# Attention with head mixing and a gated MLP: the second mixing and the product with v issued in turns of four matmuls

## The chip, the cores and the metric

One core of a Trainium2 chip. The metric is the device time of one execution in microseconds (us); a kernel's time is the median of its runs.

## The reference

Attention over 4 batches, 12 heads, 448 positions and 64 columns, with the heads mixed before and after the softmax; then RMS norm and a gated MLP.

```python
scores = scale * np.matmul(q, k.transpose(0, 1, 3, 2))
scores = np.einsum('bhij,hg->bgij', scores, w_pre)
scores = scores - np.max(scores, axis=-1, keepdims=True)
attn = np.exp(scores)
attn = attn / (np.sum(attn, axis=-1, keepdims=True) + 1e-09)
attn = np.einsum('bhij,hg->bgij', attn, w_post)
attn_out = np.matmul(attn, v)
...
rms = np.sqrt(np.mean(x * x, axis=-1, keepdims=True) + 1e-06)
xn = x / rms * rms_g
g = xn @ w_gate
silu = g * (1.0 / (1.0 + np.exp(-g)))
val = xn @ w_val
return (silu * val @ w_out).astype(np.float32)
```

## The kernel before

The kernel has two parts. `part_a` is the attention, `part_b` the MLP; the change is in `part_a` alone. All is in float32, and the order of the instructions on each engine is the order in which the program writes them.

Attention works on 16 chunks of query rows (four to a batch) and on pairs of row groups within a chunk (6, 6, 6 and 5), which makes 92 **steps**. The loop over `t` in `part_a` is a software pipeline. In step `t` TensorE gets, in this order:

- `premix` (tile `sp`): the first mixing of the heads, for the pair of step `t`, in turns with `qk_mm` (tile `qk`), the product of q and k for a chunk further on. Each has four products of 448 columns.
- `postmix` (`pm`): the second mixing, for the pair of step `t - 1`: 28 products of 60 columns, whose stationary operand is `e`, the exponentials, and whose moving operand is `wn`, the mixing weights divided by the row sums.
- `av_mm` (`av`): the product with v for a block of two chunks that was mixed before, mostly eight products of 240 or 120 columns a step. A block has twelve units (`av_at`), most steps have one; there is none in the first 13 steps.

All these products use 64 rows and 64 columns of the array (`pm` 60 rows), so four of them, one in each quadrant ("tile" of the array below), stand side by side. A float32 product shows in the profile as two matmul instructions with a weight load each.

The other engines follow in each step, in this order. ACT: `av_copy` when two units of `av` are complete (tile `xt`), two `expo` (`e`), one `qk_evac` (`st`), one half of `evac_a` (`at_all`). DVE: two `rowmax` (`nm`), one `qk_evac` (`st`), the other half of `evac_a` (`at_all`), then `norm` (`t`, `rp`). GpSimd (POOL): `wn` at the end of `norm`, and the sums of squares. In a run of steps DVE also converts the MLP's first weights (`first_w`, tile `wac`), one instruction a step ahead of `nm`.

The banks: `sp`, `qk`, `pm` and `av` have two PSUM banks each. The two banks of `av` hold two head pairs side by side (240 columns each), so they are written anew after four units:

```python
        if at_ % 2 == 0 and part != 1:
            xps[k, at_ // 2] = banks((ps_m, ps_v, ps_s)[at_ // 2] if ns[0] == NCHUNK - 1 else ps_v, "av")
```

and `done` is the list of the head pairs of `av` that the step before completed; their copies are written between `premix` and `rowmax`.

Of the kernel before, what the change touches and what calls it, by code (L numbers as in the profile page):

```python
# [16 lines left out]
B, H, S, D = 4, 12, 448, 64  # L17
# [7 lines left out]
HR = H * RH  # L25
# [9 lines left out]
HH = H // 2  # L35
ROWS = [0, 6, 1, 7, 2, 8, 3, 9, 4, 10, 5, 11]
JB = S // 64
JT = 64
JC, JP = 4, 112
# [6 lines left out]
def attention_moe(ctx: ExitStack, tc, q, k, v, wpre, wpost, mask, ident, wgv, wo, rms_g, out):  # L46
    nc = tc.nc
    NCHUNK = B * NC
# [38 lines left out]
    def load_consts():  # L87
        nc.sync.dma_start(msk.rearrange("p a r -> p (a r)"), mask)
        nc.sync.dma_start(we, wpre)
        nc.sync.dma_start(wp, wpost)  # L90
# [9 lines left out]
    kt, qt, vt, rt, sps, et, sm, wn, pm, nmx, qps, xps, xt = ({} for _ in range(13))  # L100

    def load_k(b, hp):
        t = kt[b, hp] = pq.tile([128, S], F32, name=f"k{b}_{hp}", tag=f"k{hp}", bufs=1)
        (nc.gpsimd if b else nc.sync).dma_start(t, k[b, :, hp])

    def load_q(n, hp, many=3, eng=nc.gpsimd):
        b, c = divmod(n, NC)
        if not hp:
            qt[n] = pq.tile([128, H // 2, 128], F32, name=f"q{n}", tag="q", bufs=2)
        hp = slice(hp, hp + many)  # L110
        eng.dma_start(qt[n][:, hp], q[b, :, c, hp])
# [13 lines left out]
    def banks(pl, name, many=2, at_=0):  # L125
        return [pl.tile([128, 512], F32, name=name, tag=f"{pl.name}{i}", bufs=1) for i in range(at_, at_ + many)]
# [83 lines left out]
    def postmix(n, p):  # L210
        ps = banks(ps_m, "pm")
        e, w = et.pop((n, p)), wn.pop((n, p))
        for u in range(2):
            u_ = min(u, len(e) - 1)
            for c in range(JC):
                for m in range(2) if c < JC - 1 else (u,):
                    j = min(2 * c + m, S // JT - 1) * JT
                    for v_ in range(2):
                        sl = slice(64 * v_, 64 * v_ + HR)
                        at_ = u * (JC - 1) + c if c < JC - 1 else JB - 1  # L220
                        o = ps[v_][64 * m : 64 * m + JT, : JB * HR].rearrange("p (s a i) -> p s a i", s=2, a=JB)
                        w_ = w[sl, u_].rearrange("p (s i) -> p s i", s=2)
                        nc.tensor.matmul(o[:, :, at_], e[u_][sl, j : j + JT], w_, start=True, stop=True)  # L223
        pm[n, p] = ps

    def evac_a(n, p, v_):
        if n == p == v_ == 0:
            pro_ctx.close()
            p2.append(pool(a_ctx, "p2", 2))
            p1.append(pool(a_ctx, "p1"))  # L230
        lo, hi = SLOTS[n]
        a = 2 * RH * p + RH * v_
        dst = at_all[:, lo : hi + 1 : hi - lo, :, a : a + RH]
        src = pm[n, p][v_][:, : JB * HR].rearrange("p (s x r) -> p s x r", s=2, r=RH)
        if v_:
            nc.vector.tensor_copy(dst, src)
        else:
            nc.scalar.activation(dst, src, AF.Copy)

    def heads_of(k):  # L240
        o = list(range(H // 2))
        return o[3:] + o[:3] if LATE_FIRST[k] else o
# [4 lines left out]
    def av_mm(k, at_, part):  # L247
        ns, hp = BLOCKS[k], heads_of(k)[at_]
        b, half = ns[0] // NC, 2 * hp // HH
        w = 2 * RH * PAIRS[ns[0] % NC]  # L250
        many = len(ns) * 2 * w
        if at_ % 2 == 0 and part != 1:
            xps[k, at_ // 2] = banks((ps_m, ps_v, ps_s)[at_ // 2] if ns[0] == NCHUNK - 1 else ps_v, "av")
        o = [x[:, (at_ % 2) * 240 : (at_ % 2) * 240 + many] for x in xps[k, at_ // 2]]
        sl_ = [SLOTS[n][half] for n in ns]
        a_ = at_all[:, sl_[0] : sl_[-1] + 1 : max(sl_[-1] - sl_[0], 1)].rearrange("p s (b h) i -> p s b h i", h=HH)
        for c_ in range(JC) if part is None else (2 * part, 2 * part + 1):
            for m in range(2):
                sl = slice(64 * m, 64 * m + JT)
                for j in range(2):  # L260
                    h = (2 * hp + j) % HH
                    x = o[m][64 * j : 64 * j + 64].rearrange("p (g u i) -> p g u i", u=2, i=w)
                    if c_ < JC - 1:
                        a = a_[sl, :, c_ : JB - 1 : JC - 1, h, :w]
                    else:
                        x, a = x[:, :, m], a_[sl, :, JB - 1, h, :w]
                    nc.tensor.matmul(x, vt[b, hp][sl, j, c_], a, start=(c_ == 0), stop=(c_ == JC - 1))  # L267

    def av_copy(k, i):
        ns = BLOCKS[k]  # L270
# [104 lines left out]
    first = [steps.index((n, 0)) for n in range(NCHUNK)] + [T, T + 3]  # L375
    qk_at = [[] for _ in range(T + 40)]
    av_at = [[] for _ in range(T + 40)]
# [4 lines left out]
    for blk, ns in enumerate(BLOCKS):  # L382
# [3 lines left out]
        for i, a in enumerate(units):  # L386
            t = lo + i * (hi - lo) // len(units)
# [7 lines left out]
    for n in range(NCHUNK):  # L395
        b, c = divmod(n, NC)
# [15 lines left out]
    for b in range(B - 1):  # L412
        t = first[NC * b + NC + 2] + (5 if b < B - 2 else 3)
# [3 lines left out]
    def part_a(extra):  # L417
        for j in range(H // 4):
            load_q(0, 2 * j, 2, nc.scalar)
            load_k(0, 2 * j)  # L420
            load_k(0, 2 * j + 1)
        load_consts()
        load_q(1, 0, 6, nc.sync)
        nc.vector.memset(r_all[0], 0.0)
        nc.gpsimd.memset(r_all[1], 0.0)
        nc.vector.memset(ones, 1.0)
        for hp in range(H // 2):
            alone(qk_mm(0, hp))
            for j in range(2):
                qk_evac(0, hp, j)  # L430
            if hp == 4:
                setup()
        for i, args in enumerate(held):
            (nc.gpsimd if i % 5 in (1, 3) else nc.sync).dma_start(*args)
        load_q(2, 0)
        nc.gpsimd.memset(r_all[2], 0.0)
        load_q(2, 3)
        for hp in range(AHEAD):
            alone(qk_mm(1, hp))
            for j in range(2):  # L440
                qk_evac(1, hp, j)
        busy, = banks(ps_v, "busy", 1)
        for _ in range(4):
            nc.tensor.matmul(busy[:, :S], ones, kt[0, 0], start=True, stop=True)
        nc.sync.dma_start(g_sb, rms_g)
        nc.sync.dma_start(eye, ident)
        done = []
        for t in range(T + 24):
            def back(lag):
                return steps[t - lag] if 0 <= t - lag < T else None  # L450

            if t == first[NCHUNK - 1]:
                qk_ctx.close()
                start_b()
            for f, *a in jobs_at[t]:
                f(*a)
            while stored:
                x_store(*stored.pop(0))
            done = [(k, i // 2) for k, i, part in (av_at[t - 1] if t else []) if i % 2 and part != 0]
            sp = premix(*back(0)) if back(0) else []  # L460
            if qk_at[t]:
                qk = qk_mm(*qk_at[t][0])
                if any(f is sq_all and not a[1] for f, *a in last_at[t - 1]):
                    qk.reverse()
                order = sp[:1] + qk[1:] + sp[1:] + qk[:1]
            else:
                order = sp
            for x in order:
                for y in x:
                    y()  # L470
            for a in done:
                av_copy(*a)
            if back(0):
                rowmax(*back(0))
                expo(*back(0))
            if back(1):
                postmix(*back(1))
            for a in av_at[t]:
                av_mm(*a)
            for a in qk_at[t][:1]:  # L480
                for j in range(2):
                    qk_evac(*a, j)
            if back(1):
                for v_ in range(2):
                    evac_a(*back(1), v_)
            if back(0) and t >= T - 2:
                norm(*back(0))
            for op in sum_ops[: 1 if t < first[NCHUNK - 2] else 2 if t <= T else 4]:
                op()
                sum_ops.pop(0)  # L490
            if back(0) and t < T - 2:
                norm(*back(0))
            for a in qk_at[t][1:]:
                alone(qk_mm(*a))
                for j in range(2):
                    qk_evac(*a, j)
            for f, *a in last_at[t]:
                f(*a)
            for a in done:
                x_sum(*a)  # L500
            extra(t - T, bool(done))
            if t >= T + 4 and not done and not stored and not sum_ops and not any(av_at[t:]):
                break
# [108 lines left out]
    w, xs, wos, fac, hs, hr, keep = {}, {}, {}, {}, {}, [], {}  # L612
# [382 lines left out]
```

## Time and profile before

| | |
|---|---|
| median of 3 runs | 865.17 us (863.83 to 868.22) |
| the profiled execution | 866.41 us, with a span of 864.6 us |
| TensorE (PE) | 827.3 us busy, 96% of the span, 10900 matmuls |
| its weight loads (PEld) | 710.8 us, 10900 |
| VectorE (DVE) | 600.4 us |
| ScalarE (ACT) | 390.4 us |
| GpSimd (POOL) | 437.6 us |

Busy time is the time in which an engine had at least one instruction in flight; TensorE overlaps matmuls, so its share says little about holes. The attention part with the change in it runs up to about 347 us of the span, the MLP from there.

### The profile page before, as it was taken

Reading aid. Unit: us, or ns where it says so; the run is one execution under the profiler, and the core shown is the slowest. Engines: PE = TensorE matmul, PEld = TensorE weight load, DVE = VectorE, ACT = ScalarE, POOL = GpSimd, SP = SyncE. Lnnn points to the kernel's source line nnn. Section 1 sums busy time; section 2 is a strip of 40 time slices with the busy share of each in tenths; the row PEclk is TensorE's granted clock in tenths of the full one; section 3 lists DMA queues with packets and bytes.
Section 4 is the critical chain, followed back from the end, with each engine's and each line's share of the span. In section 5 each row is a group of like instructions: output and inputs, shape, how many; then the busy total and the mean of one; then the engine's idle time right before and its main releaser. Section 6 shows DMA issues by size and latency. Waiting matters only on the chain.

```text
span 864.6 us, 26550 instructions
## 1 busy us (share of the span) xinstructions
PE 827.3 (96%) x10900; PEld 710.8 (82%) x10900; DVE 600.4 (69%) x985; ACT 390.4 (45%) x869; POOL 437.6 (51%) x537
## 2 busy tenths in 40 slices
PE   7899999998899898999999999999999999999998
PEld 2556777777678686799999999999999999999997
DVE  5676787887677666778655858576668359978461
ACT  3677777777677676732211222222121235554310
POOL 7233455554555347935634646365356369573100
PEclk9999999999999999999999999999999999999999
DMA  7777678667756653744634535535354246664541
GB/s 203 202 229 206 202 226 237 213 196 220 223 156 178 184 165 111 231 155 118 215 100 153 139 119 154 179 98 170 105 180 138 64 134 195 201 189 134 170 129 64
DMA packets 77547, 144.53 MB, mean 167 GB/s; under 512 B 10495, under 2 KB 66845, under 8 KB 77427
## 3 DMA queue, kind: packets, MB, share of 16 engines
q1 hardware_dynamic: 72814, 129.19, 49.0%
q0 software_dynamic: 3648, 11.31, 4.8%
q10 hardware_dynamic: 965, 2.34, 0.8%
q8 instruction: 86, 1.41, 0.7%
q14 instruction: 34, 0.28, 0.1%
HBM read 72.03 MB, written 31.21 MB: 119 GB/s over the span
## 4 chain that ended last, share of the span: by engine, by line
PE 90%; DMA 3%; issue 3%; POOL 2%; DVE 1%; ACT 0%; ACTq 0%; SPq 0%; POOLq 0%; DVEq 0%
PE pm L223 9%; PE qk L134 8%; PE sp L182 7%; PE av L267 7%; PE pg L608 6%; PE pg L609 6%; PE pv L609 6%; PE pg L610 6%; PE pv L610 6%; PE pv L608 6%; PE po L610 6%; PE po L609 6%; PE po L608 6%; DMA r<-st 3%; POOL d L358 0%
## 5 line engine op out<-in xcount | busy, mean ns | idle before, releaser
L182 PE MATMUL sp<-r,wk_pre 64*64 64x448 f32 x720 | 162.7, 539 | 4.4 <-DMA r<-st 2.0
L134 PE MATMUL qk<-k,q 64*64 64x448 f32 x768 | 154.6, 560 | 5.9 <-DMA q<-in_q 4.1
L196 ACT ACTIVATE e<-sp,nm 128x448 f32<-128x448 f32 x180 | 114.4, 638 | 88.4 <-DVE nm L189 86.2
L223 PEld LDWEIGHTS pm<-wn,e 60*64 60x64 f32 x5152 | 110.1, 134 | 50.9 <-POOL wn L208 21.5
L189 DVE TENSOR_REDUCE nm<-sp 128x1 f32<-128x448 f32 x180 | 111.5, 622 | 56.2 <-PE sp L182 25.3
L208 POOL TENSOR_SCALAR wn<-wk,rp 128x60 f32<-128x60 f32 x180 | 55.8, 322 | 162.4 <-DVE rp L205 143.1
L223 PE MATMUL pm<-wn,e 60*64 60x60 f32 x5152 | 109.5, 220 | 18.0 <-issue 14.9
L267 PE MATMUL av<-at_all,v 64*64 64x240 f32 (+4 forms) x1728 | 95.1, 319 | 3.6 <-issue 3.6
L608 PE MATMUL pg<-x,wh 128*128 128x448 f32 x264 | 96.8, 367 | 0.0
L609 PE MATMUL pv<-x,wh 128*128 128x448 f32 x264 | 96.4, 365 | 0.0
L608 PE MATMUL pv<-x,wh 128*128 128x448 f32 x264 | 96.4, 365 | 0.0
L610 PE MATMUL pg<-x,wl 128*128 128x448 f32 x264 | 96.4, 365 | 0.0
L610 PE MATMUL pv<-x,wl 128*128 128x448 f32 x264 | 96.4, 365 | 0.0
L609 PE MATMUL pg<-x,wh 128*128 128x448 f32 x264 | 96.4, 365 | 0.0
L595 DVE TENSOR_TENSOR x<-hraw,x 128x448 fp32r<-128x448 f32 x84 | 91.6, 1137 | 6.8 <-ACT x L594 6.8
L609 PE MATMUL po<-x,fac 128*128 128x448 f32 x252 | 92.1, 365 | 0.0
L608 PE MATMUL po<-x,fac 128*128 128x448 f32 x252 | 92.0, 365 | 0.0
L610 PE MATMUL po<-x,fac 128*128 128x448 f32 x252 | 92.0, 365 | 0.0
L642 POOL TENSOR_TENSOR sg<-sg,u 128x448 f32<-128x448 f32 x36 | 48.1, 1335 | 83.0 <-DVE u L638 43.5
L637 ACT ACTIVATE sg<-g 128x448 f32<-128x448 f32 x48 | 27.4, 571 | 129.2 <-DVE g L636 118.6
L182 PEld LDWEIGHTS sp<-r,wk_pre 64*64 64x64 f32 x720 | 62.4, 133 | 22.2 <-issue 9.6
L638 DVE TENSOR_TENSOR u<-pv,ry 128x448 f32<-128x448 f32 x48 | 29.9, 623 | 69.1 <-PE pv L610 60.6
(118 smaller groups left out, 1709.9 us busy)
## 6 DMA issues: line engine op xcount, KB each, us to landing
r<-st SPq DMA_DIRECT2D x117, 210.0 KB
hraw<-td SPq DMA_DIRECT2D x84, 224.0 KB
wraw<-in_wgv SPq DMA_DIRECT2D x20, 768.0 KB
td<-keep SPq DMA_DIRECT2D x48, 224.0 KB
wraw<-in_wo SPq DMA_DIRECT2D x12, 768.0 KB
r<-st SPq DMA_DIRECT2D x44, 175.0 KB
v<-in_v SPq DMA_DIRECT2D x24, 256.0 KB
q<-in_q POOLq DMA_DIRECT2D x28, 192.0 KB, 5.1
```

Source lines behind the costliest of these rows:

```text
L134: nc.tensor.matmul(ps[j][m, :S], qt[n][sl, hp, m], kt[n // NC, hp][sl], start=True, stop=True)
L182: nc.tensor.matmul(o, wk_pre[sl], rt[n][sl, 2 * p + v_], start=True, stop=True)
L189: nc.vector.tensor_reduce(t, ps[:, :S], AX.X, ALU.max, negate=True)
L196: nc.scalar.activation(e, ps[:, :S], AF.Exp, bias=nmx.pop((n, p, u)), accum_out=sm[n, p][:, u : u + 1])
L208: nc.gpsimd.tensor_scalar(wn[n, p][:, u], wk, r[:, u : u + 1], 1.0, ALU.mult, ALU.mult)
L223: nc.tensor.matmul(o[:, :, at_], e[u_][sl, j : j + JT], w_, start=True, stop=True)
L267: nc.tensor.matmul(x, vt[b, hp][sl, j, c_], a, start=(c_ == 0), stop=(c_ == JC - 1))
L595: nc.vector.tensor_tensor(lo, raw, hi.bitcast(F32), ALU.subtract)
L608: nc.tensor.matmul(ps, a, xh[:, kk], start=(kk == 0), stop=False)
L609: nc.tensor.matmul(ps, a, xl_[:, kk], start=False, stop=False)
L610: nc.tensor.matmul(ps, a2, xh[:, kk], start=False, stop=(kk == KT - 1))
L642: nc.gpsimd.tensor_tensor(h, sg, u, ALU.mult)
```

## The change

`postmix` no longer issues its products but returns them as seven groups of four: a group is one turn over the four tiles of the array, six for the pairs of column blocks and one for the last blocks of both halves. `av_mm` returns its products in groups of four as well, one for each column block. The loop puts the two lists in one order: each group has a place between 0 and 1 in its list, and the groups are issued by place, `av` ahead of `pm` where the places are equal. With two `av` groups the order is `av`, four `pm`, `av`, three `pm`. From the first step of the last chunk on, all `pm` groups come first and all `av` groups after them.

```diff
     def postmix(n, p):
         ps = banks(ps_m, "pm")
         e, w = et.pop((n, p)), wn.pop((n, p))
-        for u in range(2):
+        def one(u, c, m, v_):
             u_ = min(u, len(e) - 1)
-            for c in range(JC):
-                for m in range(2) if c < JC - 1 else (u,):
-                    j = min(2 * c + m, S // JT - 1) * JT
-                    for v_ in range(2):
...
+            nc.tensor.matmul(o[:, :, at_], e[u_][sl, j : j + JT], w_, start=True, stop=True)
+
+        fours = [[(u, c, m) for m in range(2)] for u in range(2) for c in range(JC - 1)]
+        fours.append([(u, JC - 1, u) for u in range(2)])
         pm[n, p] = ps
+        return [[lambda x=x, v_=v_: one(*x, v_) for x in f for v_ in range(2)] for f in fours]
...
+        cs = range(JC) if part is None else (2 * part, 2 * part + 1)
+        return [[lambda x=(c_, m, j): one(*x) for m in range(2) for j in range(2)] for c_ in cs]
...
-            if back(1):
-                postmix(*back(1))
-            for a in av_at[t]:
-                av_mm(*a)
+            pm_ = postmix(*back(1)) if back(1) else []
+            av_ = [x for a in av_at[t] for x in av_mm(*a)]
+            if t < first[NCHUNK - 1]:
+                both_ = [(i / len(x), k, f) for k, x in enumerate((av_, pm_)) for i, f in enumerate(x)]
+                fours = [f for _, _, f in sorted(both_, key=lambda x: x[:2])]
+            else:
+                fours = pm_ + av_
+            for f in fours:
+                for x in f:
+                    x()
```

What stood on TensorE in a step in which the `av` banks are written anew (the second pair of chunk 8, with the waits that an instruction carries; `Activation_49` is ACT's semaphore, `Pool_49` GpSimd's):

```order
L134 MATMUL qk<-k_4_2988,q_3163 64x448 [waits Activation_49]
L134 MATMUL qk<-k_4_2988,q_3163 64x448
L223 MATMUL pm<-wn,e 64x2x30 [waits Activation_49,Pool_49]
L223 MATMUL pm<-wn,e 64x2x30 [waits DVE_49]
L223 MATMUL pm<-wn,e 64x2x30 x12
L223 MATMUL pm<-wn,e 64x2x30 [waits Pool_49]
L223 MATMUL pm<-wn,e 64x2x30 x13
L267 MATMUL av<-at_all,v_3_2179 64x240 [waits Activation_49]
L267 MATMUL av<-at_all,v_3_2179 64x240
L267 MATMUL av<-at_all,v_3_2179 64x240 [waits Activation_49]
L267 MATMUL av<-at_all,v_3_2179 64x240 x5
```

And what stands there now:

```order
L134 MATMUL qk<-k_4_2988,q_3163 64x448 [waits Activation_49]
L134 MATMUL qk<-k_4_2988,q_3163 64x448
L266 MATMUL av<-at_all,v_3_2179 64x240 [waits DVE_49,Activation_49]
L266 MATMUL av<-at_all,v_3_2179 64x240
L266 MATMUL av<-at_all,v_3_2179 64x240 [waits PE_49,Activation_49]
L266 MATMUL av<-at_all,v_3_2179 64x240
L220 MATMUL pm<-wn,e 64x2x30 [waits PE_49,Pool_49]
L220 MATMUL pm<-wn,e 64x2x30 [waits PE_49]
L220 MATMUL pm<-wn,e 64x2x30 x10
L220 MATMUL pm<-wn,e 64x2x30 [waits Pool_49]
L220 MATMUL pm<-wn,e 64x2x30 x3
L266 MATMUL av<-at_all,v_3_2179 64x240 x4
```

The first and the third `av` product, each the first to write its bank, with their waits for ACT's copies, moved from behind the 28 `pm` products to ahead of them; the last twelve `pm` products follow the second `av` group.

The step after it, in which no bank is written anew, before:

```order
L134 MATMUL qk<-k_5_3085,q_3163 64x448 [waits Activation_49]
L134 MATMUL qk<-k_5_3085,q_3163 64x448
L223 MATMUL pm<-wn,e 64x2x30 [waits Activation_49,Pool_49]
L223 MATMUL pm<-wn,e 64x2x30 [waits DVE_49]
L223 MATMUL pm<-wn,e 64x2x30 x12
L223 MATMUL pm<-wn,e 64x2x30 [waits Pool_49]
L223 MATMUL pm<-wn,e 64x2x30 x13
L267 MATMUL av<-at_all,v_3_2179 64x240 x4
L267 MATMUL av<-at_all,v_3_2179 64x2x60 x4
```

and a step of the same kind now (the first pair of chunk 8):

```order
L134 MATMUL qk<-k_3_2908,q_3163 64x448 [waits Activation_49]
L134 MATMUL qk<-k_3_2908,q_3163 64x448
L266 MATMUL av<-at_all,v_2_2985 64x240 x4
L220 MATMUL pm<-wn,e 64x2x30 [waits Activation_49,Pool_49]
L220 MATMUL pm<-wn,e 64x2x30 [waits DVE_49]
L220 MATMUL pm<-wn,e 64x2x30 x14
L266 MATMUL av<-at_all,v_2_2985 64x2x60 x4
L220 MATMUL pm<-wn,e 64x2x30 x12
```

Here the first four `av` products carry no wait, and the wait for `wn` stands behind them; the end of `pm` moved to the end of the step. The orders of DVE, ACT, POOL and SP are the same before and now.

## Rows read from the trace of the kernel before

**Rows 1.** The page: busy time, share of the span, instructions; granted TensorE clock in tenths.

```profile
PE 827.3 (96%) x10900; PEld 710.8 (82%) x10900; DVE 600.4 (69%) x985; ACT 390.4 (45%) x869; POOL 437.6 (51%) x537
...
PEclk9999999999999999999999999999999999999999
```

**Rows 2.** Timeline of TensorE, one ordinary step: start us, us, engine, line, operation, count.

```profile
255.25 0.54 PE L182 MATMUL sp<-r,wk_pre 64*64 64x448 f32 x1
...
255.63 0.54 PE L182 MATMUL sp<-r,wk_pre 64*64 64x448 f32 x1
...
256.75 1.03 PE L223 MATMUL pm<-wn,e 60*64 60x60 f32 x50
257.57 0.37 PE L267 MATMUL av<-at_all,v 64*64 64x240 f32 x1
...
257.69 0.22 PE L223 MATMUL pm<-wn,e 60*64 60x60 f32 x2
...
258.19 0.54 PE L182 MATMUL sp<-r,wk_pre 64*64 64x448 f32 x1
```

**Rows 3.** TensorE's waits from 60 to 347 us: us in total, times, longest.

```profile
PE pm L223 <- issue: 11.1, 9, 2.1
PE av L267 <- issue: 3.6, 4, 1.4
PE pm L223 <- POOL wn L208: 2.8, 4, 1.1
```

**Rows 4.** Timeline of TensorE in a step that writes the `av` banks anew.

```profile
183.21 0.59 PE L182 MATMUL sp<-r,wk_pre 64*64 64x448 f32 x2
...
184.78 1.01 PE L223 MATMUL pm<-wn,e 60*64 60x60 f32 x51
185.59 0.37 PE L267 MATMUL av<-at_all,v 64*64 64x240 f32 x1
185.62 0.28 PE L223 MATMUL pm<-wn,e 60*64 60x60 f32 x5
```

**Rows 5.** Timeline of ACT in the same step.

```profile
183.39 0.53 ACT L156 ACTIVATE st<-qk 128x448 f32<-128x448 f32 x1
183.81 0.61 ACT L238 ACTIVATE at_all<-pm 128x420 f32<-128x420 f32 x1
184.28 1.04 ACT L276 ACTIVATE xt<-av 128x480 f32<-128x480 f32 x2
```

**Rows 6.** Timeline, the end of a late `pm` and DVE's copy of it.

```profile
254.50 0.28 PE L223 MATMUL pm<-wn,e 60*64 60x60 f32 x3
...
254.85 0.60 DVE L236 COPY at_all<-pm 128x420 f32<-128x420 f32 x1 [0.87 <-PE pm L223]
```

**Rows 7.** Groups of instructions from 60 to 347 us: count, busy us, mean ns.

```profile
L276 ACT ACTIVATE xt<-av 128x480 f32<-128x480 f32 (+1 forms) x28 | 13.7, 551 | 0.9 <-PE av L267 0.7 <-POOL sum L305 0.2
...
L278 ACT ACTIVATE xt<-av 128x240 f32<-128x240 f32 x18 | 7.0, 388 | 0.0
...
L516 DVE SCALAR_TENSOR_TENSOR wac<-wraw,wac 128x384 int32<-128x384 int32 x4 | 2.2, 538 | 0.0
```

**Rows 8.** Timeline of DVE from the copy of `pm` to the next `nm`.

```profile
186.18 0.58 DVE L236 COPY at_all<-pm 128x420 f32<-128x420 f32 x1
...
187.03 0.34 DVE L513 TENSOR_SCALAR wac<-wraw 128x384 int32<-128x384 int32 x1
187.50 1.39 DVE L189 TENSOR_REDUCE nm<-sp 128x1 f32<-128x448 f32 x2
```

**Rows 9.** Timeline, ACT behind that `nm`, and the start of the next step on TensorE.

```profile
188.22 0.64 ACT L196 ACTIVATE e<-sp,nm 128x448 f32<-128x448 f32 x1 [0.74 <-DVE nm L189]
...
189.61 0.53 ACT L156 ACTIVATE st<-qk 128x448 f32<-128x448 f32 x1
...
189.34 0.54 PE L182 MATMUL sp<-r,wk_pre 64*64 64x448 f32 x1
```

More of the change, by code (lines that the diff above doesn't have):

```diff
@@ L212, in postmix @@
         e, w = et.pop((n, p)), wn.pop((n, p))
-        for u in range(2):
+        def one(u, c, m, v_):
             u_ = min(u, len(e) - 1)
-            for c in range(JC):
-                for m in range(2) if c < JC - 1 else (u,):
-                    j = min(2 * c + m, S // JT - 1) * JT
-                    for v_ in range(2):
[L219 to L223, printed above, removed]
+            j = min(2 * c + m, S // JT - 1) * JT
+            sl = slice(64 * v_, 64 * v_ + HR)
+            at_ = u * (JC - 1) + c if c < JC - 1 else JB - 1
+            o = ps[v_][64 * m : 64 * m + JT, : JB * HR].rearrange("p (s a i) -> p s a i", s=2, a=JB)
+            w_ = w[sl, u_].rearrange("p (s i) -> p s i", s=2)
+            nc.tensor.matmul(o[:, :, at_], e[u_][sl, j : j + JT], w_, start=True, stop=True)
+        fours = [[(u, c, m) for m in range(2)] for u in range(2) for c in range(JC - 1)]
+        fours.append([(u, JC - 1, u) for u in range(2)])
         pm[n, p] = ps
+        return [[lambda x=x, v_=v_: one(*x, v_) for x in f for v_ in range(2)] for f in fours]
     def evac_a(n, p, v_):
@@ L256, in av_mm, with one @@
         a_ = at_all[:, sl_[0] : sl_[-1] + 1 : max(sl_[-1] - sl_[0], 1)].rearrange("p s (b h) i -> p s b h i", h=HH)
[L257 to L267, printed above, removed]
+        def one(c_, m, j):
+            sl = slice(64 * m, 64 * m + JT)
+            h = (2 * hp + j) % HH
+            x = o[m][64 * j : 64 * j + 64].rearrange("p (g u i) -> p g u i", u=2, i=w)
+            if c_ < JC - 1:
+                a = a_[sl, :, c_ : JB - 1 : JC - 1, h, :w]
+            else:
+                x, a = x[:, :, m], a_[sl, :, JB - 1, h, :w]
+            nc.tensor.matmul(x, vt[b, hp][sl, j, c_], a, start=(c_ == 0), stop=(c_ == JC - 1))
+        cs = range(JC) if part is None else (2 * part, 2 * part + 1)
+        return [[lambda x=(c_, m, j): one(*x) for m in range(2) for j in range(2)] for c_ in cs]
     def av_copy(k, i):
@@ L475, in part_a @@
                 expo(*back(0))
-            if back(1):
-                postmix(*back(1))
-            for a in av_at[t]:
-                av_mm(*a)
+            pm_ = postmix(*back(1)) if back(1) else []
[3 more added lines that the diff above has]
+                fours = [f for _, _, f in sorted(both_, key=lambda x: x[:2])]
+            else:
+                fours = pm_ + av_
+            for f in fours:
+                for x in f:
+                    x()
             for a in qk_at[t][:1]:
```

## The prediction

> **What bounds the kernel now.** I read the page first: TensorE is busy 96% of the span and its granted clock is full in every slice, so no time is to be had from the clock [rows 1]. A busy TensorE says little, so I took one ordinary step of the attention part from the timeline [rows 2]. The scores (`sp` and `qk`) begin at 255.25 us, the second mixing (`pm`) at 256.75, the product with v (`av`) at 257.57, the next step's `sp` at 258.19: 1.50 + 0.82 + 0.62 = 2.94 us and nothing between. The two `sp` rows of one tile, 255.25 and 255.63, are one pass of 448 columns, 0.38 us, or 0.85 ns a column; four passes a tile are the 1.50 us. So the four 64x64 tiles stream without a hole, and in such a step **the order of the three blocks cannot matter: 2.94 us is their sum**. (A step whose `av` part has only 240-column products takes 0.2 us more.)
>
> One block is not at the streaming rate: 56 `pm` instructions in 0.82 us on four tiles are 58.6 ns each in a tile, where 60 columns at 0.85 ns would be 51. The 7.6 ns more, 14 times a step, are 0.11 us.
>
> What is lost beside the streaming is in the list of waits [rows 3]. Most of it has the releaser "issue", 14.7 us in 13 stops before `pm` and `av`: TensorE waited for nothing that the profile shows, and no operand is late there. Only 2.8 us, in four stops, is `pm` waiting for `wn` of GpSimd.
>
> **The change part by part.** It removes and adds no instruction. In 74 steps (chunk 2, pair 1 to the end of chunk 14) it puts the first four `av` products ahead of `pm`, and in the 66 of them with eight `av` products the other four behind the fourth of the seven `pm` groups; the order on ACT, DVE, POOL and SP stays. In the 13 steps before there is no `av`, and from the last chunk on `pm` leads as before; the new order inside `pm` costs nothing there, since its 56 instructions share the four tiles evenly either way.
>
> *Weight loads.* A `pm` product that follows an `av` product in its tile has its weights loaded under some 0.2 us of streaming. Before, one of 14 a tile followed a long product; now two do. That gains 7.6 ns a step, 0.6 us over 74. If weaving hid all of them it would be 0.11 x 74 = 8 us. I take 0.6, because twelve of fourteen still follow another `pm` product in their tile.
>
> *The wait for wn.* `av` ahead gives GpSimd half of the `av` block, 0.31 to 0.41 us, more. Between 0 and 2.8 us; at most 0.4 in each of the four stops, so -1.6 us.
>
> *The wait for the bank.* Two banks hold the `av` sums; every fourth step ACT copies both out (`xt`) and the same step's first `av` products overwrite them. In the step at 183.21 us [rows 4] `pm` begins at 184.78 and `av` at 185.59. ACT [rows 5] does `st` at 183.39, `at_all` at 183.81 and then the copies, from 184.28 for 1.04 us, to 185.32. Today the copies end 0.27 us before `av` needs the banks, and **the work that hides them is `pm`**. With `av` first, its third product (the second bank) is wanted at 184.78 and cannot start before 185.32: 0.54 us, and some 0.07 us until the signal is seen, which is what DVE needs from the end of the last `pm` to its copy, 254.78 to 254.85 [rows 6]. Behind that product the whole `pm` stands in TensorE's queue, so nothing fills the hole. Bounds: 0 where the copies happen to be early, and 0.81 us (the whole cover, 184.78 to 185.59). I take 0.61, since ACT's run from `st` to the copies is fixed by the same score block that `pm` follows. The number of such steps: the window has 14 pairs of `xt` at L276 and 9 at L278 [rows 7], of which three belong to the last chunk; 20 are left. Where TensorE stood in "issue" just ahead, ACT has caught up; I count 16. **16 x 0.6 = 9.6 us.**
>
> *The later end of pm.* `pm` now ends with the step, 0.62 or 0.82 us later. DVE's `at_all` copy waits for that end, and behind it on DVE stand `t`, `rp`, any weight conversion (`wac`) and the next `nm`; behind `nm` on ACT stand `e` and `st`, and the next step's `qk` waits for `st`. In the step above the last `pm` row ends at 185.90 [rows 4]; 0.82 later is 186.72, and DVE can start at 186.79 instead of 186.18 [rows 8]. From there to the next instruction after `rp` it takes 0.85 us (186.18 to 187.03), so 187.64. Without a conversion `nm` is then 0.14 us later than the 187.50 of today; behind a 0.34 us conversion (187.03) it starts near 187.98, 0.48 us later. Does that reach TensorE? ACT's `e` follows at 188.22 and its `st` ends at 189.61 + 0.53 = 190.14, while the next step, begun at 189.34, reaches the `qk` that needs this bank after two passes, at 190.10 [rows 9]. No slack there; the alternate, longer step has 0.2 us of it. So two neighbouring steps lose 0.48 + 0.28 with conversions, 0.38 each, and 0.14 + 0 without, 0.07 each. The conversions are five lines of four like L516 [rows 7], 20 steps; about six of them are bank steps, already lengthened. 14 x 0.38 + 38 x 0.07 = 8.0 us. Bounds: 0 if DVE and ACT take it up in idle time, and 0.48 in each of 20 and 0.14 in each of 54 steps, 17 us. I take the middle value, because the chain has slack in every second step.
>
> *The stops in "issue".* The same instructions are issued, so I keep the stops; but whatever they wait for outside the trace comes at its own time, and a step that is longer by some 0.24 us (17.6 over 74) leaves less to wait. Between 0 and all 14.7; 13 stops of 0.24 give -3 us.
>
> One rule of the skill speaks against the change. In [rows 2] `pm` has 60 rows and 64 columns, `av` 64 and 64, and `av` begins in one tile at 257.57 while `pm` still starts in another at 257.69: nothing empties in between. The Trainium skill, TensorEngine Tiling (Array Packing), section Key Properties, says that a change of tiling mode drains the engine, while other tiles of one mode run independently. By the row there is no change of mode here; were it one, the rival below would hold.
>
> **Sum.** -0.6 - 1.6 + 9.6 + 8.0 - 3.0 = +12.4 us. The profiled execution took 866.41 us (864.6 of span); 878.8. The median of the runs is 1.2 us under it, so **about 878 us**, 1.5% slower. Its own range is 870 to 886.
>
> **Rivals.**
> 1. *Cover instead of waits: faster.* `av` ahead hides all of `wn` (2.8 us) and the long products all of `pm`'s excess (8 us), while the copies are early. The time is 865.2 - 10.8 = 854 at best, near 859 if half of it comes. For it: the excess is there in every step. Against: the copies end 0.54 us into `pm`. It decides if ACT's copies end before 184.78 in the step shown, that is half a microsecond earlier. Chance 0.07.
> 2. *It doesn't do what it says: no change.* The waits for the bank fall into time that TensorE now loses in "issue", and DVE catches up there. 9.6 + 8.0 less 14.7 and 2.2 is about 0, 866 us. For it: the stops are long, up to 2.1 us. Against: they are 13 among 74 steps, and a lost step ahead of a stop helps only where the two meet. Chance 0.11.
> 3. *The chain closes on itself: much slower.* The late `pm` makes the whole circle `pm`, DVE, ACT, `qk` the bound of every step, and each bank step pays the full 0.81 us: 16.2 + 17 = 33 us, less the 5 us above; 893 us, or 885 to 895. For it: DVE has little idle time in the steps with conversions. Against: slack of 0.2 us in each longer step. Chance 0.16.
> 4. *Tiles that must empty at each switch.* Two more switches a step, each the 0.22 us that a `pm` instruction takes [rows 2], 74 times: 33 us, 899 us. (That is the skill's rule above, if it held.) Against: the overlap at 257.57. Chance 0.02.
>
> **How the numbers follow.** The forecast has 0.64. A change within 0.5% (4.3 us, about what a measurement of this kernel can tell from none) holds rival 2 and a thin edge of the forecast; slower by more holds nearly all of the forecast and rivals 3 and 4. So faster 0.07, same 0.12, slower 0.81. From 868 to 889 us lie the forecast and the nearer half of rival 3; outside are rival 1, most of rival 2, the far half of rival 3 and rival 4, in all about 0.2 or a little more.
>
> **What the new profile would show.** Right: new waits before `av` released by ACT's `xt`, about 0.5 us each and near 16 to 20 of them; `pm` without waits for `wn`; DVE's `at_all` waiting for `pm` in most steps, and more idle time of `qk` behind `st`; `pm` still 0.82 us of work for 56 instructions; "issue" near 12 us; everything behind the attention part only shifted. Wrong: `av` starting at once in the bank steps, `pm` at 51 ns a tile, or fewer stops in "issue" by more than 5 us. The forecast fails most easily in the 8.0 us, which rest on one chain through three engines, and in the stops, which no row explains.

## The result, and the profile after

The changed kernel takes 873.5 us (median of 19 runs, 865.93 to 878.57), the kernel before 864.68 us in its 19 runs beside it (855.77 to 870.73). The ratio is 1.0117, with a 95% interval of 1.009 to 1.0143: **slower by 1.2%, about 10.1 us** (7.8 to 12.4). Forecast were 878 us and +12.4 us. Differences in microseconds here and below are worked out from the ratio and its interval; the two medians can lie further apart or closer (8.8 us here; for E2 they are 4.4 us apart, where the ratio gives 1.9). The profiled execution took 872.12 us with a span of 870.3.

The page of the changed kernel: busy time and instructions, the clock, and the queue that brings instructions (packets, MB, share of 16 engines).

```profile
PE 838.1 (96%) x10900; PEld 707.4 (81%) x10900; DVE 599.2 (69%) x985; ACT 389.3 (45%) x869; POOL 438.3 (50%) x537
...
PEclk9999999999999999999999999999999999999999
...
q8 instruction: 86, 1.41, 0.7%
```

The instructions are the same in number and the clock is as full as in [rows 1]. TensorE's busy time went up by 10.8 us with the same work: busy means "something in flight", and a wait in one tile counts as busy while another tile still works. The turns as such don't raise it: E6 below takes as many and has 828.8 us, where the kernel before has 827.3.

TensorE's waits from 60 to 355 us (us in total, times, longest), to lay beside [rows 3]:

```profile
PE pm L220 <- issue: 7.6, 6, 2.8
PE pm L220 <- POOL wn L208: 3.8, 6, 1.2
PE av L266 <- issue: 2.7, 3, 2.3
...
PE av L266 <- ACT xt L278: 0.2, 1, 0.2
```

This list hides the loss. A wait of `av` for `xt` appears once, with 0.2 us. The reason is that "idle" is counted for the whole array, and a matmul that is still in flight in some tile covers the wait. The weight loads are the better witness, since a wait sits on the load that precedes a product:

```profile
PEld av L266 <- ACT xt L278: 9.4, 21, 1.0
PEld pm L220 <- POOL wn L208: 9.1, 11, 1.8
...
PEld av L266 <- ACT xt L282: 6.9, 15, 0.7
```

Now there are 36 waits of `av` weight loads for ACT's copies, 16.3 us together, in all 20 steps that write the banks anew (both banks in 16 of them); in the kernel before there is none. Not all of it is lost, because the first bank's wait lies partly under the `qk` products.

One such step in full, the one of [rows 4], now at 190.04 us. TensorE:

```profile
190.04 0.54 PE L182 MATMUL sp<-r,wk_pre 64*64 64x448 f32 x1
...
191.83 0.88 PE L266 MATMUL av<-at_all,v 64*64 64x240 f32 x6
192.40 0.35 PE L220 MATMUL pm<-wn,e 60*64 60x60 f32 x5
192.54 0.37 PE L266 MATMUL av<-at_all,v 64*64 64x240 f32 x2
...
193.04 0.37 PE L266 MATMUL av<-at_all,v 64*64 64x240 f32 x1
193.09 0.23 PE L220 MATMUL pm<-wn,e 60*64 60x60 f32 x3
...
193.80 0.54 PE L182 MATMUL sp<-r,wk_pre 64*64 64x448 f32 x1
```

The weight loads of the same step, and what they waited for:

```profile
191.83 0.20 PEld L266 LDWEIGHTS av<-at_all,v 64*64 64x64 f32 x4 [0.60 <-ACT xt L278]
192.29 0.20 PEld L266 LDWEIGHTS av<-at_all,v 64*64 64x64 f32 x4 [0.27 <-ACT xt L278]
192.37 0.32 PEld L220 LDWEIGHTS pm<-wn,e 60*64 60x64 f32 x8
```

And ACT, as in [rows 5]:

```profile
190.32 0.53 ACT L156 ACTIVATE st<-qk 128x448 f32<-128x448 f32 x1
...
190.74 0.61 ACT L239 ACTIVATE at_all<-pm 128x420 f32<-128x420 f32 x1
...
191.21 1.03 ACT L278 ACTIVATE xt<-av 128x480 f32<-128x480 f32 x2
```

ACT ends its copies at 192.24. The third `av` product, which writes the second bank, has its weights loaded from 192.29. The first `pm` load follows at 192.37, since it stands behind it in the queue, although `wn` and `e` were there. The step lasts 190.04 to 193.80, 3.76 us, where [rows 4] has 183.21 to 186.41, 3.20: 0.56 us more; the prediction had 0.61.

### The profile page after: what moved, and what is told of

Read it like the earlier page. It is cut to its first block, busy times and chain, and to the rows that moved or that the text cites. A ratio compares the mean times of both kernels' runs of the same rounds, so it can differ in the third digit from the quotient of the medians.

```text
span 870.3 us, 26541 instructions
## 1 busy us (share of the span) xinstructions
PE 838.1 (96%) x10900; PEld 707.4 (81%) x10900; DVE 599.2 (69%) x985; ACT 389.3 (45%) x869; POOL 438.3 (50%) x537
## 3 DMA queue, kind: packets, MB, share of 16 engines
q8 instruction: 86, 1.41, 0.7%
## 4 chain that ended last, share of the span: by engine, by line
PE 90%; POOL 3%; issue 2%; DMA 2%; DVE 1%; ACT 1%; ACTq 0%; SPq 0%; DVEq 0%; POOLq 0%
PE qk L134 10%; PE pm L220 8%; PE av L266 7%; PE sp L182 7%; PE pg L616 6%; PE pg L617 6%; PE pv L617 6%; PE pg L618 6%; PE pv L618 6%; PE pv L616 6%; PE po L616 6%; PE po L617 6%; PE po L618 6%; DMA r<-st 2%; POOL xt L292 1%
## 5 line engine op out<-in xcount | busy, mean ns | idle before, releaser
L134 PE MATMUL qk<-k,q 64*64 64x448 f32 x768 | 152.0, 563 | 6.1 <-DMA q<-in_q 4.2
L220 PEld LDWEIGHTS pm<-wn,e 60*64 60x64 f32 x5152 | 126.7, 134 | 25.9 <-POOL wn L208 11.1
L220 PE MATMUL pm<-wn,e 60*64 60x60 f32 x5152 | 130.9, 219 | 11.5 <-issue 7.6
L266 PE MATMUL av<-at_all,v 64*64 64x240 f32 (+4 forms) x1728 | 127.4, 321 | 3.0 <-issue 2.7
L189 DVE TENSOR_REDUCE nm<-sp 128x1 f32<-128x448 f32 x180 | 108.9, 616 | 22.0 <-PE sp L182 14.1
L266 PEld LDWEIGHTS av<-at_all,v 64*64 64x64 f32 x1728 | 74.9, 133 | 35.1 <-issue 12.5
L237 DVE COPY at_all<-pm 128x420 f32<-128x420 f32 x92 | 54.9, 597 | 63.5 <-PE pm L220 63.1
```

The source lines that it names most:

```text
L134: nc.tensor.matmul(ps[j][m, :S], qt[n][sl, hp, m], kt[n // NC, hp][sl], start=True, stop=True)
L189: nc.vector.tensor_reduce(t, ps[:, :S], AX.X, ALU.max, negate=True)
```

## The experiments

All were timed beside the kernel before; no experiment has the number E4 or E5. E1, E2, E3 and E6 share their runs of before (863.95 us, 29 runs), E7 to E10 another set (863.05 us, 28 runs).

**E1: the groups without the weaving.** `pm` in its new order of seven groups, all of it ahead of `av`.

```diff
-            if t < first[NCHUNK - 1]:
+            if t < first[NCHUNK - 1] and False:
```

> The second mixing in its new groups of four, but all of it ahead of the product with v in every step, as before the change. Theory (bank wait and late end of the mixing cost the time): both causes are gone, so the time is that of before within 2 us, and the list of waits has no weight load of av waiting for xt. Rival (the new order inside the mixing is itself slower, for instance by the earlier wait for the second half of wn): some 5 to 10 us above before, with new waits of pm for wn.

Measured: 866.88 us, ratio 1.0008 (0.9978 to 1.0038). The new order inside `pm` costs nothing that can be measured; the interval ends at 3.3 us.

**E2: woven but in the bank steps.** In the 20 steps in which `av` writes a bank that ACT is copying out, `pm` leads.

```diff
+            fresh = bool(done) and any(i % 2 == 0 and part != 1 for _, i, part in av_at[t])
-            if t < first[NCHUNK - 1]:
+            if t < first[NCHUNK - 1] and not fresh:
```

> Woven as in the change, but not in the 20 steps in which av writes its banks anew behind ACT's copies; there pm leads. Theory: the bank wait is most of the loss, about 0.5 us in each of 20 steps, so this is 9 to 10 us under the change and within 0 to 3 us of before. Rival 1 (the late end of pm closes the circle through DVE and ACT): most of the loss stays, 6 us or more above before. Rival 2 (each switch between the two kinds of product costs something, spread evenly): 54 of 74 steps are left, so 7 us above before.

Measured: 868.38 us, ratio 1.0022 (0.9992 to 1.0051), that is 1.9 us above before (-0.7 to 4.4). Most of the loss is gone when 20 of the 74 steps are no longer woven, so neither an even cost of switching (7 us) nor the closed circle (6 us or more) holds.

**E3: woven in the bank steps alone.**

```diff
-            if t < first[NCHUNK - 1]:
+            if t < first[NCHUNK - 1] and fresh:
```

> Woven only in the 20 steps in which av writes its banks anew. Theory: 8 to 10 us above before, and the weight loads of av wait for xt about as long in total as in the change (16 us over both banks). Rivals 1 and 2 (circle, or even cost of switching): 2 to 4 us above before.

Measured: 872.69 us, ratio 1.0085 (1.0052 to 1.0118): 7.3 us above before (4.5 to 10.2). The weight loads of E3 wait for the copies nearly as long as those of the full change:

```profile
PEld av L266 <- ACT xt L278: 7.6, 17, 0.7
PEld av L266 <- ACT xt L282: 6.5, 16, 0.6
```

14.1 us in 33 waits, against 16.3 in 36. So weaving the bank steps alone costs most of what the change costs.

E2 and E3 don't split the change into two clean parts, although 7.3 + 1.9 us come near its 10.1. Each changes 20 times from one order to the other, and a step in which `pm` leads behind a woven step pays for it: `pm` ended late, so `at_all`, the sums behind it on DVE and `wn` are late, and no `av` products stand ahead of `pm` to cover that. A bank step of E2, begun at 239.86 us:

```profile
240.26 0.60 DVE L237 COPY at_all<-pm 128x420 f32<-128x420 f32 x1 [0.29 <-PE pm L220]
...
241.30 0.60 POOL L208 TENSOR_SCALAR wn<-wk,rp 128x60 f32<-128x60 f32 x2 [0.99 <-DVE rp L205]
...
241.66 0.91 PEld L220 LDWEIGHTS pm<-wn,e 60*64 60x64 f32 x56 [0.65 <-POOL wn L208]
```

`pm` starts 1.80 us into this step and the step lasts 3.48; in the kernel before it is 1.58 and 3.21. In the median E2's bank steps are 0.25 us longer than the same steps before and 0.29 longer than in E1; in E3 it is the step behind each bank step, by 0.31 to 0.32 (steps with a stop of TensorE left out). The change as a whole has no such seams inside its 74 steps.

**E6: the same weaving with pm leading.** The sort gives each `av` group the place at its end, not at its start, so the order with two `av` groups is four `pm` groups, `av`, three `pm` groups, `av`, and `pm` leads in all 74 steps.

```diff
-                both_ = [(i / len(x), k, f) for k, x in enumerate((av_, pm_)) for i, f in enumerate(x)]
+                both_ = [((i + 1 - k) / len(x), k, f) for k, x in enumerate((av_, pm_)) for i, f in enumerate(x)]
```

> The same weaving in all 74 steps with the same number of switches, but pm leading: four groups of pm, one of av, three of pm, one of av. Theory: av comes 0.46 us later in the step, so all but about 0.1 us of each bank wait is covered, and pm ends only half an av block later than before; 0 to 3 us above before. Rival (switching between the kinds costs, or weaving lets the tiles run empty): as slow as the change, 8 to 10 us above before. Other rival (weaving as such gains under the cover): 2 to 5 us below before.

Measured: 867.48 us, ratio 1.0019 (0.9989 to 1.005): as before, within what can be told. The number of switches between the two kinds of product is that of the change. TensorE in a bank step of E6, begun at 99.23 us:

```profile
100.78 0.72 PE L220 MATMUL pm<-wn,e 60*64 60x60 f32 x32
101.29 0.66 PE L266 MATMUL av<-at_all,v 64*64 64x240 f32 x8
101.70 0.54 PE L220 MATMUL pm<-wn,e 60*64 60x60 f32 x22
```

and ACT's copies in it:

```profile
100.24 1.03 ACT L278 ACTIVATE xt<-av 128x480 f32<-128x480 f32 x2
```

They end at 101.27, just ahead of `av` at 101.29: four groups of `pm` are cover enough, and in the 20 bank steps only one weight load of `av` waits for a copy, for 0.2 us. So weaving as such costs nothing that can be measured; what costs is `av` ahead of `pm`. (E6 also ends `pm` half an `av` block earlier than the change; E7 and E8 look at that.)

**E7 and E8: more work on DVE.** The prediction gave 8.0 us to a circle through `pm`, DVE, ACT and `qk`. E2 left at most some 4 us for it, seams included. To make it show, both kernels put two small DVE instructions into each of the 74 steps where the weight conversions stand; E7 with `pm` ahead as in E1, E8 woven as in E2.

```diff
             for f, *a in jobs_at[t]:
                 f(*a)
+            if first[2] < t < first[NCHUNK - 1]:
+                for _ in range(2):
+                    nc.vector.tensor_scalar(idle, idle, 1.0, None, ALU.mult)
```

> The kernel of the first experiment (pm ahead of av in every step) with two small DVE instructions more in each of the 74 steps, some 0.4 us, at the place where the weight conversions stand. It is the base for the next run. DVE then has about 3.2 us of work in a step of 2.9 to 3.2, and 3.5 in the 20 steps with conversions: some 8 to 16 us above before by either theory.

> The same DVE load, with the weaving in the 54 steps that write no bank anew. If the late end of pm closes the circle through DVE, ACT and qk wherever DVE has something ahead of nm (0.38 us a step, as the prediction had it), this is about 14 us or more above the run before it, since now all 54 steps have such work. If the circle has slack that the prediction missed (the second experiment measured about 2 us in place of 8), it is 0 to 5 us above the run before it.

Measured: E7 873.63 us, ratio 1.0103 (1.0068 to 1.0139); E8 873.06 us, 1.0102 (1.0071 to 1.0133). The extra DVE work costs 9 us in both, and weaving adds nothing to it (E8 less E7 is -0.7 us by their mean times, with 2.9 us either way). DVE's groups in E8, from 60 to 347 us (count, busy, mean ns, idle before and what ended it), show that the load was there and that DVE did wait for `pm`:

```profile
L238 DVE COPY at_all<-pm 128x420 f32<-128x420 f32 x81 | 48.2, 596 | 32.5 <-PE pm L221 31.8
...
L463 DVE TENSOR_SCALAR idle<-idle 128x8 f32<-128x8 f32 x148 | 27.6, 187 | 2.7 <-DVE idle L463 0.2
```

That is 31.8 us of waiting in 51 steps, where E7 has 15.0 in 15, and no time lost by it: the circle is not what the prediction took it for.

**E9: the copies earlier on ACT.** The change in full, with the `xt` copies written at the end of the step before, ahead of `at_all`.

```diff
-            for a in done:
-                av_copy(*a)
+            if t >= first[NCHUNK - 1]:
+                for a in done:
+                    if a not in xt:
+                        av_copy(*a)
...
+            if t < first[NCHUNK - 1]:
+                for k, i, part in av_at[t]:
+                    if i % 2 and part != 0:
+                        av_copy(k, i // 2)
             if back(1):
                 for v_ in range(2):
                     evac_a(*back(1), v_)
```

> The change in full, but ACT copies the av banks at the end of the step before, ahead of its at_all copy and not behind it. Theory (av waits for ACT to reach the copies): they end some 0.45 us earlier, av waits about 0.15 us in place of 0.55, but pm, next in the queue, then waits for at_all, which ends where the copies ended, some 0.3 us; so 2 to 5 us under the change and 4 to 8 above before. Rival (the wait is for something else than ACT's place in its queue): as the change, 10 us above before.

Measured: 869.18 us, ratio 1.0068 (1.0034 to 1.0102): 5.9 us above before (2.9 to 8.8), where the change is 10.1 above its own runs of before. TensorE in a bank step of E9:

```profile
76.94 0.74 PE L266 MATMUL av<-at_all,v 64*64 64x240 f32 x8
77.64 0.69 PE L220 MATMUL pm<-wn,e 60*64 60x60 f32 x32
```

and ACT:

```profile
75.96 1.04 ACT L278 ACTIVATE xt<-av 128x480 f32<-128x480 f32 x2
76.86 0.63 ACT L239 ACTIVATE at_all<-pm 128x420 f32<-128x420 f32 x1
```

The copies end at 77.00, and the first `av` group runs from 76.94 without a hole. But `pm` starts 0.70 us after it, where an ordinary step has 0.41 (195.31 to 195.72 in the changed kernel): it now waits for `at_all`, which ends at 77.49. The profile puts this wait down to `wn`, but `wn` had ended at 77.32, and in twelve of the bank steps the first `pm` load follows 0.11 to 0.13 us behind `at_all`. In five bank steps `av` itself waits for `at_all`, which E9 put behind the copies:

```profile
PEld av L266 <- ACT at_all L239: 5.0, 5, 1.1
```

The wait changed its place and shrank: a bank step is 0.25 to 0.40 us longer than an unwoven one in the median, where the change has 0.50 to 0.62. So it is ACT's queue that sets it.

**E10: where the stops come from.** The change with 64 TensorE instructions more at the start, timed once.

```diff
-        for _ in range(4):
+        for _ in range(20):
             nc.tensor.matmul(busy[:, :S], ones, kt[0, 0], start=True, stop=True)
```

> The change with 16 more full-array matmuls at the start, 64 TensorE instructions (each matmul is two with a weight load each). In the traces so far nearly every stop of TensorE without a releaser ends at the 191st instruction of a run of 256 counted from the first. If the stops are instructions that arrive late, they still end at the 191st, so at other places of the program. If they belong to a place in the program or to an operand, they now end at the 255th. The time says nothing here; the start is longer by up to 12 us where TensorE waited anyway.

Measured: 883.67 us, one run; the start is 11.7 us longer than in the changed kernel. The waits of E10 from 60 to 360 us:

```profile
PE pm L220 <- issue: 9.7, 7, 3.0
...
PE av L266 <- issue: 2.6, 2, 1.4
```

I numbered TensorE's instructions (matmuls, weight loads and those that only wait for a semaphore) in the order of their starts, counted on modulo 256, and looked where gaps of over 0.6 us between two starts end, from 60 to 347 us. In the kernel before, 15 of 20 end at 193; in the changed kernel 8 of 14; in E10 10 of 14, again at 193, and none at 1, where a shift of 64 would have put them. (The expectation's "191st" is the same place, counted a little differently.) These stops belong to the count of instructions and not to a place in the program.

## Why the prediction was right, point by point

**The streaming cannot change with the order: right.** E1 and E6 lie within 0.2% of before, with intervals that end at 0.4 and 0.5%. Of the 8 us that weaving could at best have hidden in `pm`'s weight loads nothing is to be seen.

**The wait for the bank: right in place and cause, near in size.** It is 0.56 us in the step shown, against 0.61. Over the whole stretch the same step can be laid beside itself in two traces, where neither has a stop of TensorE over 0.6 us in it. Of the 20 bank steps 12 can be compared with the kernel before and 11 with E1: the change makes them 0.50 and 0.62 us longer in the median. So the price per step was right, and the count of 16 rather low, since all 20 steps have the wait: 10 to 12 us by this estimate, against the forecast 9.6. E3 measured 7.3 us (4.5 to 10.2) with its seams; that is less than the 13 to 15 us that its bank steps and seams would add up to by the steps without a stop, and its trace has only 7.0 us of stops before `pm` and `av` where the kernel before has 14.7. That the stops give the rest back is likely but was not tried by itself.

**The later end of pm: the step that failed.** 8.0 us were forecast; E2 holds it, its seams and all gains together at 1.9 us (-0.7 to 4.4), and E8 against E7 shows none. Step by step, the 54 steps of the change that write no bank are 0.03 us longer in the median (0.06 to 0.07 in the mean, some 4 us together), those of them with conversions 0.10 to 0.14 where 0.38 was forecast. The delay itself is there. DVE in the changed kernel, the step with a conversion that answers to [rows 8]:

```profile
194.22 0.60 DVE L237 COPY at_all<-pm 128x420 f32<-128x420 f32 x1 [1.03 <-PE pm L220]
...
195.08 0.34 DVE L521 TENSOR_SCALAR wac<-wraw 128x384 int32<-128x384 int32 x1
195.34 1.15 DVE L189 TENSOR_REDUCE nm<-sp 128x1 f32<-128x448 f32 x2
...
197.16 0.61 DVE L237 COPY at_all<-pm 128x420 f32<-128x420 f32 x1
```

and what follows it on ACT and TensorE, as in [rows 9]:

```profile
196.05 0.64 ACT L196 ACTIVATE e<-sp,nm 128x448 f32<-128x448 f32 x1 [1.26 <-DVE nm L189]
...
197.28 0.54 ACT L156 ACTIVATE st<-qk 128x448 f32<-128x448 f32 x1
...
196.83 0.59 PE L182 MATMUL sp<-r,wk_pre 64*64 64x448 f32 x2
...
200.31 0.55 PE L182 MATMUL sp<-r,wk_pre 64*64 64x448 f32 x2
```

The step began at 193.80, so `nm` starts 1.54 us into it, where before it was 187.50 - 186.41 = 1.09: 0.45 us late (forecast 0.48). But from `nm` to `st` it is 1.94 us now and was 2.11, because the two `nm` take 1.15 us and took 1.39: before, the last `sp` products started at 187.69, while the first `nm` ran, and now they start at 195.10, ahead of both. That takes up 0.17. The step itself is 0.10 longer (3.03 against 2.93), and so `st` ends 0.99 us into the next step, against 0.80. That step is 3.48 us long, against 3.29. So the two steps lose 0.29 us together and not 0.76, and in the following one DVE has no wait for `pm` at all (197.16). The prediction counted the full delay in each of two neighbours, and left out that the chain had a wait of its own to give.

The list of DVE's waits tells the same of the whole stretch (60 to 355 us), first before, then now:

```profile
DVE nm L189 <- PE qk L134: 21.1, 35, 2.0
DVE nm L189 <- PE sp L182: 20.3, 59, 1.7
DVE at_all L236 <- PE pm L223: 16.5, 17, 2.1
...
DVE at_all L237 <- PE pm L220: 63.1, 75, 3.8
DVE nm L189 <- PE sp L182: 7.0, 16, 2.5
DVE nm L189 <- PE qk L134: 1.9, 2, 1.7
```

DVE waits for `pm` in 75 steps, as forecast; its waits ahead of `nm` are 8.9 us and 18 in number, where they were 41.4 and 94. Idle time that `nm` used to have is now in front of `at_all`.

**The wait for wn: no gain shown.** 1.6 us were forecast. TensorE waits 3.8 us for `wn` now, in a slightly longer stretch than the 2.8 us of [rows 3]. In the list of weight loads the wait halved, from 18.8 us in 48 to 9.1 in 11, but such waits need not cost: E6 has 42.3 us of them and is as fast as before.

**The stops: open in size.** -3 us were forecast. The stops before `pm` and `av` sum to 10.3 us in the changed kernel, 14.7 before, 12.3 in E10 and 14.3 in E6 (6.3 before `pm`, 8.0 before `av`), single executions all; that scatter is larger than the term.

**The switch of tiles.** In the step at 190.04 `pm` starts in one tile at 193.09 while `av` is in flight in another since 193.04, and E6 has the change's switches for at most 4.3 us. The Trainium skill, TensorEngine Tiling (Array Packing), section Key Properties, reserves the drain for a change of tiling mode; by these rows 60 and 64 rows are one mode here.

In sum the main term was right, and it alone comes near the measured 10.1 us. That the whole sum did too (12.4) is in part luck: the chain was counted some 4 to 6 us too dear and the bank steps up to some 2 too cheap, and of the 4.6 us credited to `wn` and the stops none is shown by a timing.

## What to carry to other kernels

Before a block of work is moved ahead on an engine, look for what it waited behind: a block that seems only to stand in the way can be the cover of another queue's work. If the blocks already stream without holes, a new order of them has nothing to give, and only its waits count. For a late link in a chain through several engines, subtract the waits that the chain already contains, and don't charge two neighbouring steps with one delay. An experiment that applies a change in some steps only has costs of its own at the seams; look for them before its result is taken as a share of the whole.

## What the hardware showed that was not expected

- Most stops of TensorE with no releaser, 0.6 to over 3 us long, end at one place of each 256 of its instructions (193, whatever the order of the program and after a shift by 64). The instruction queue brings 86 packets of 1.41 MB together, 16.4 KB each, which would be 64 bytes for each of 256 instructions. It fits instructions that arrive late; that the queue's packets cause the stops was not tried by itself.
- Products in different tiles of the array start out of the order of the program: in [rows 2] an `av` product starts at 257.57 and `pm` products, which stand ahead of it, at 257.69.
- A wait of a product can be missing from the list of TensorE's matmuls and stand in that of its weight loads: 0.2 us in one wait there, 16.3 us in 36 here.
